# Entering the first round of a staged token-mixing kernel in eight steps instead of six

## The chip, the cores and the metric

The kernel runs on one NeuronCore of a Trainium2 chip. The metric is the device time of one execution in microseconds (us), taken as the median of several runs. The engines are called as the profile calls them: PE (TensorE, matrix products), DVE (VectorE), ACT (ScalarE), POOL (GpSimd) and SP (SyncE, which here only issues DMAs); "PEld" is PE's loading of weights.

## The reference

Eight sequences of 4224 tokens with 192 channels go through a causal seven-tap convolution, whose weights are a softmax per head, and then through a token-mixing layer:

```python
x  = causal_conv(x, softmax(weight))          # 8 heads of 24 channels, 7 taps
th = x @ w_theta
y  = einsum('ts,bsd->btd', w_tok_r, x*cos(th)) + einsum('ts,bsd->btd', w_tok_i, x*sin(th))
u  = x + y
out = u + relu(u @ w_ch)
```

Nearly all the arithmetic is in the two 4224 x 4224 token mixes, `w_tok_r` and `w_tok_i`, each applied to 8 x 192 = 1536 columns.

## The kernel before

**Tiles.** The 4224 input tokens are cut into 33 *chunks* (`NK`) of 128, and the 4224 output tokens into 33 *row blocks* of 128. Row blocks are handled in pairs, which gives 17 *units* (`NU`): 16 pairs and one single block. Every chunk must meet every unit once.

**What a chunk needs before it can be mixed** (class `Chunk`): its x tokens are loaded by POOL's queue, and a short history of 16 tokens per quarter is copied by SP's queue from the chunk before (tile `xw`); two convolutions on PE (`conv`, L216) with their evacuation by ACT or DVE; a store of the convolved x (`store`, SP); twelve PE transposes (`transpose`, L170); two channel mixes on PE (`theta`, L146), each followed by two sines on ACT (L291); two products on DVE (`product`, L297); four subtractions on DVE (`sums`, L306). The result, seven half-width operands, stays in SBUF in one of 11 `z` buffers (`NW` = 11).

**Steps.** Time is cut into *steps* (class `Step`). In a step one unit is mixed with all the chunks that are active in it, `n` of them. A chunk enters at step `start[k]`, stays for 17 steps, and then leaves its `z` buffer to the chunk that comes 11 later; so there are three *rounds* of 11 chunks. The list `start` decides how many chunks are active in each step. With

```python
base = [0, 0, 1, 1, 2, 3, 3, 4, 4, 5, 5]
start = [base[k % NW] + (NU + 1) * (k // NW) for k in range(NK)]
```

the first six steps have n = 2, 4, 5, 7, 9, 11, most steps have 11, and where one round gives way to the next n falls to 9 or 10 for six steps (17 to 22 and 35 to 40). The last five steps have 9, 7, 6, 4, 2. There are 58 steps, and `shift` puts the single block on the last one.

**The mix of one pair of row blocks** is a seven-product scheme: four token-weight tiles are turned on DVE from the loaded `st` (`turn`, L387) and four combinations of them are formed on DVE (`wsum`, L399); then seven *runs* of n *products* each go to PE, a product being two matmuls of 384 columns (L536). After each run the sum in PSUM is given to the row block's accumulator `pv` (`give`): by DVE (L461), or in the first round for four of the seven by ACT (L459). PSUM holds two such sums at a time. In steps 0 and 1 (`plain`) eight runs without combinations take the place of the seven.

**Between steps** the accumulators of a row block go to DRAM and come back 17 steps later (`part`, 768 KB each way per row block, SP's queue, L549 and L425). The token weights of step t+2 are loaded during step t (`load_w`, L374): four DMAs each for `w_tok_r` and `w_tok_i` on POOL's queue, into two `st` buffers. `xw` and `pv` share six buffers (tag `big`).

**The order of the work** is written by hand. `Step.mix` yields before every product, and at set places within the step (in sevenths of it) runs its events: the next step's turns and sums, loads, the tasks of the chunks that enter at the next step (`Chunk.tasks`, places in `step_events`), and outputs in the last 17 steps. The residual x is added to each row block once: by POOL in the step before a visit (`load_x`, `add_x`, L439) or by an accumulating DMA into `part` (`add_ahead`, L448). `quiet` says which visits of the second round may take it.

The first 11 chunks are not prepared through `step_events` but by the loop at the end of the kernel, its *entry passes* i = 1 to 12. Pass i issues the convolutions and transposes of chunk i and the channel mixes and products of chunk i-1, and between them calls `between`, which lets `more` take products from the stream of steps as long as these need no chunk above `ready[0]` = i-2. Before, a pass takes up to 11 products (2+1+2+1+2+1+1+1), and chunk i+3 is loaded in pass i, chunks 0 to 5 ahead of the passes. In pass 1, `idle` matmuls on noise keep PE busy.

Of the kernel before, what the change touches and what calls it, by code (L numbers as in the profile page):

```python
# [16 lines left out]
def kernel(  # L17
# [34 lines left out]
    NK = S // P  # L52
# [7 lines left out]
    NU = (NT + 1) // 2  # L60
    NW = 11
    PC = 512
    NP = 4

    base = [0, 0, 1, 1, 2, 3, 3, 4, 4, 5, 5]
    assert len(base) == NW
    start = [base[k % NW] + (NU + 1) * (k // NW) for k in range(NK)]
    NSTEP = start[-1] + NU
    shift = (NU - 1 - (NSTEP - 1)) % NU

# [14 lines left out]
    def pe(ins):  # L85
        return in_order("pe", ins)
# [96 lines left out]
    class Chunk:  # L183


        def __init__(self, k, before=None):
            self.k = k
            self.xw = wk.tile([2 * WR, 2, B, D], F16, name="xw", tag="big", bufs=6)
            for a in range(NQ):
                h, lo = a // 2, (a % 2) * WR  # L190
                t0 = token(k, a)
                hist = self.xw[lo : lo + HALO, h, :, :]
                if before is not None:
                    nc.sync.dma_start(  # L194
                        out=hist, in_=before.xw[lo + Q : lo + Q + HALO, h, :, :]
                    )
                elif t0 == 0:
                    nc.vector.memset(hist, 0.0)
                else:
                    lo, t0 = lo - HALO, t0 - HALO  # L200
                lo += HALO
                n = (a % 2 + 1) * WR - lo
                nc.gpsimd.dma_start(  # L203
                    out=self.xw[lo : lo + n, h, :, :],
                    in_=x[:, t0 : t0 + n, :].rearrange("b s d -> s b d"),
                )
# [117 lines left out]
    def load_chunk(k):  # L324
        if k < NK and k not in chunks:
            chunks[k] = Chunk(k, before=chunks[k - 1] if k % NW else None)

    def active(t):
        return [k for k in range(NK) if start[k] <= t < start[k] + NU]

    def unit(t):
        return (t + shift) % NU

    class Step:


        def __init__(self, t):
            self.t, self.u, self.ks = t, unit(t), active(t)
            self.n = len(self.ks)
            self.tbs = [tb for tb in (2 * self.u, 2 * self.u + 1) if tb < NT]  # L340
            self.pair = len(self.tbs) == 2
            self.first = t < NU
            self.final = t + NU >= NSTEP
            self.late = self.final and self.n < NW
            visits = [v for v in range(NU, NSTEP) if v % NU == t % NU]
            quiet = [v for v in visits if start[2 * NW - 1] < v <= 2 * NU]
            self.adds, self.ahead = [], []
            for i, tb in enumerate(self.tbs):
                known = self.known(tb)
                if t not in ([v for v in quiet if known < v - 1] or visits[-1:])[:1]:  # L350
                    continue
                if not self.late:
                    self.adds.append(i)
                else:
                    far = known <= start[2 * NW - 1]
                    self.ahead.append((i, 2 * NU - NW + 2 * (t % NU) if far else start[-1],
                                       (t // NU - 1 - far) % 2))
            self.plain = self.first and self.pair and self.n <= NP
            self.time = 0.324 * self.n * (8 if self.plain else 7 if self.pair else 5 if self.n <= 2 else 4)
            self.closing = False  # L360
            self.st, self.w, self.xr, self.ub, self.uT, self.pv = {}, {}, {}, {}, {}, []
# [274 lines left out]
    steps = [Step(t) for t in range(NSTEP)]  # L636
# [75 lines left out]
    for a in range(2):  # L712
        nc.gpsimd.affine_select(
            out=sel, in_=sel, pattern=[[1, Q - 1 + 2 * WR]], channel_multiplier=-1,
            base=-(Q - 1 + HALO - KS + 1 + a * WR), compare_op=ALU.not_equal, fill=1.0,
# [13 lines left out]
    def idle(n):  # L729
        for _ in range(n):  # L730
            pe(nc.tensor.matmul(
                spare[:, 0, 0:BH], lhsT=noise[:, 0:P], rhs=noise, start=True, stop=True
            ))
# [30 lines left out]
    for q in range(Q):  # L764
# [3 lines left out]
            start=True, stop=True,  # L768
# [16 lines left out]
    flow = stream()  # L785
    need = [None]

    def more(n):

        for i in range(n):  # L790
            if need[0] is None:
                need[0] = next(flow, NK)
            if need[0] > ready[0]:
                return n - i
            need[0] = next(flow, NK)
        return 0

    steps[0].load_rows()
# [4 lines left out]
    for m in (1, 2):  # L803
        steps[1].load_w(m)
    load_chunk(4)
    load_chunk(5)
    for g in range(NG):
        chunks[0].conv_batches(g)
    idle(2)
# [2 lines left out]
    for i in range(1, NW + 2):  # L812
        ch = chunks.get(i) if i < NW else None
        old = chunks[i - 1] if i <= NW else None

        def between(n):
            left = more(n)
            if i < 3:
                idle(min(left, 2) if i == 1 else 0)

        if ch:
            ch.conv(0)
        between(2)
        if old:
            old.theta(0)
        ready[0] = i - 2
        between(1)
        if ch:
            ch.conv(1)
        between(2)  # L830
        if old:
            old.theta(1)
        if i in (1, 3):
            for name in ("11", "21"):
                steps[i // 2].turn(name)
        if i + 3 < NW:
            load_chunk(i + 3)
        between(1)
        if i == 1:
            for first in (Z11, Z21):  # L840
                old.product(first, slice(0, 1))
        if ch:
            ch.transpose()
        if i == 1:
            for first in (Z11, Z21):
                old.product(first, slice(1, 2))
        elif old:
            old.product(Z11)
        between(2)
        if i > 1 and old:  # L850
            old.product(Z21)
        if i in (1, 3):
            for name in ("12", "22"):
                steps[i // 2].turn(name)
        between(1)
        if old and start[i - 1] > NPS:
            old.sums(0)
        between(1)
        if old and start[i - 1] > NPS:
            old.sums(1)  # L860
        between(1)
    ready[0] = NK
    for _ in flow:
        pass
# [31 lines left out]
```

## Time and profile before

| | us |
|---|---|
| median of 3 runs (1435.09 to 1443.39) | 1437.17 |
| the profiled execution | 1437.8 |
| its span, first to last instruction | 1436.0 |
| PE busy in the span | 1409.4 (98%) |
| DVE busy | 973.0 (68%) |
| POOL busy | 434.3 (30%) |
| ACT busy | 310.6 (22%) |

The profile is of one execution. Its time is 1.8 us longer than its span, and 0.6 us above the median of the runs. Line numbers such as L536 are lines of the kernel before. The granted PE clock was 0.999 on the mean. PE's busy time counts the whole latency of an isolated instruction, so a busy PE may still be issuing below its best rate. [...]

### The profile page before, as it was taken

What the parts mean: (1) busy time and instruction counts of PE and PEld (TensorE: products, weight loads), DVE (VectorE), ACT (ScalarE), POOL (GpSimd) and SP (SyncE); (2) the same over time, 40 slices, a digit from 0 to 9 for tenths busy, and PEclk for the clock granted to TensorE, in tenths of its full rate; (3) what the DMA queues carried; (4) which work ended last, traced back from release to release, by engine and by line L of the source; (5) the groups of instructions that cost most, each with busy time, mean ns of one, the idle gap of its engine ahead of it and who ended that gap; (6) DMA issues with size and microseconds to landing.
All of it is one profiled execution on the core that took longest, in us unless ns stands there. A gap on an engine that the chain in (4) does not pass through costs nothing.

```text
span 1436.0 us, 23771 instructions
## 1 busy us (share of the span) xinstructions
PE 1409.4 (98%) x9829; PEld 889.7 (62%) x9829; DVE 973.0 (68%) x1046; ACT 310.6 (22%) x374; POOL 434.3 (30%) x655
## 2 busy tenths in 40 slices
PE   8889999999999999999999999999999999999997
PEld 5556666666666666666666666666566666666665
DVE  6893554545548787866665657877777677767676
ACT  5851101111124244000000004335100110010133
POOL 8511211111233332532333343233323123213110
PEclk9999999999999999999999999999999999999999
DMA  9975766564799999898899889999999999999894
GB/s 193 234 164 132 147 125 128 100 151 89 147 232 227 231 236 239 209 256 177 232 236 229 229 157 243 231 198 255 248 206 216 215 206 220 203 202 197 166 214 136
DMA packets 272045, 281.99 MB, mean 196 GB/s; under 512 B 106688, under 2 KB 240192, under 8 KB 271936
## 3 DMA queue, kind: packets, MB, share of 16 engines
q0 software_dynamic: 162464, 92.15, 48.8%
q1 hardware_dynamic: 71840, 178.88, 35.4%
q10 hardware_dynamic: 37632, 9.44, 4.5%
q8 instruction: 77, 1.26, 0.4%
q14 instruction: 32, 0.26, 0.1%
HBM read 245.49 MB, written 108.13 MB: 246 GB/s over the span
## 4 chain that ended last, share of the span: by engine, by line
PE 92%; DMA 2%; DVE 2%; ACT 1%; SPq 1%; issue 1%; POOL 0%; DVEq 0%; ACTq 0%; POOLq 0%
PE y L536 84%; PE v L146 5%; PE tp L170 1%; PE pc L216 1%; ACT z L291 1%; DMA xw<-in_x_dram 1%; DMA xw<-xw 1%; SPq L194 1%; DVE pv L461 0%; DVE z L306 0%; DVE pv L585 0%; DMA part<-pv 0%; DMA st<-in_moe_w_tok_r_dram 0%; DMA wsb<-in_weight_dram 0%; DVE wt L399 0%
## 5 line engine op out<-in xcount | busy, mean ns | idle before, releaser
L536 PE MATMUL y<-z,wt 128*128 128x384 f16 x7672 | 1282.4, 326 | 6.4 <-DVE pv L461 5.3
L536 PEld LDWEIGHTS <-wt 128*128 128x128 f16 x7672 | 743.7, 98 | 482.6 <-issue 6.3
L461 DVE TENSOR_TENSOR pv<-y,pv 128x768 f32<-128x768 f32 x317 | 302.5, 954 | 323.9 <-PE y L536 284.0
L387 DVE STREAM_TRANSPOSE wt<-st 128x1408 f16<-128x1408 f16 (+7 forms) x224 | 327.5, 1465 | 51.0 <-PE y L536 38.3
L374 POOL DMA_DIRECT2D st<-in_moe_w_tok_r_dram x232 | 132.3, 578 | 463.5 <-DVE wt L387 451.8
L374 POOL DMA_DIRECT2D st<-in_moe_w_tok_i_dram x232 | 132.4, 579 | 405.0 <-DVE wt L387 396.5
L399 DVE TENSOR_TENSOR wt<-wt 128x1408 f16<-128x1408 f16 (+6 forms) x208 | 173.4, 834 | 40.5 <-PE y L536 38.3
L156 ACT ACTIVATE z<-pc 128x768 f16<-128x768 f32 (+1 forms) x62 | 47.5, 803 | 387.0 <-PE pc L216 378.4
L156 ACT ACTIVATE ub<-pv 128x768 f16<-128x768 f32 x63 | 50.2, 836 | 343.6 <-DVE pv L461 315.9
L459 ACT ACTIVATE pv<-y 128x768 f32<-128x768 f32 x66 | 53.7, 814 | 280.5 <-PE y L536 280.5
L146 PEld LDWEIGHTS <-uT 128*128 128x128 f16 x1056 | 90.6, 98 | 23.8 <-issue 5.9
L439 POOL TENSOR_TENSOR pv<-pv,xr 128x1536 f32<-128x1536 f32 x24 | 74.5, 3103 | 66.2 <-issue 26.7
L203 POOL DMA_DIRECT2D xw<-in_x_dram x132 | 76.3, 587 | 27.1 <-issue 7.0
L585 DVE SCALAR_TENSOR_TENSOR pv<-v,pv 128x768 f32<-128x768 f32 (+1 forms) x67 | 62.8, 942 | 24.9 <-PE v L146 24.5
L306 DVE TENSOR_TENSOR z<-z 128x768 f16<-128x768 f16 x132 | 71.2, 552 | 2.2
L291 ACT ACTIVATE z<-v,half_pi 128x768 f16<-128x768 f32 x66 | 59.6, 903 | 56.4 <-PE v L146 55.7
L156 ACT ACTIVATE uT<-tp 128x1536 f16<-128x1536 f16 (+1 forms) x47 | 56.5, 1208 | 47.3 <-PE tp L170 47.3
L297 DVE TENSOR_TENSOR z<-z 128x1536 f16<-128x1536 f16 (+1 forms) x68 | 60.6, 926 | 4.3 <-ACT z L291 4.2
L146 PE MATMUL v<-wth,uT 128*128 128x192 f16 x528 | 54.4, 246 | 2.7 <-ACT z L291 2.1
L146 PE MATMUL v<-wch,uT 128*128 128x192 f16 x528 | 54.3, 246 | 1.3 <-DVE pv L585 0.7
L291 ACT ACTIVATE z<-v 128x768 f16<-128x768 f32 x66 | 53.2, 806 | 0.0
L216 PE MATMUL pc<-xw,bands 96*64 96x192 f16 x512 | 30.4, 251 | 5.4 <-DMA st<-in_moe_w_tok_r_dram 2.7
(45 smaller groups left out, 144.8 us busy)
## 6 DMA issues: line engine op xcount, KB each, us to landing
part<-pv SPq DMA_DIRECT2D x79, 768.0 KB, 4.3
pv<-part SPq DMA_DIRECT2D x79, 768.0 KB, 6.0
out_dram<-pv SPq DMA_DIRECT2D x65, 384.0 KB, 4.5
st<-in_moe_w_tok_r_dram POOLq DMA_DIRECT2D x136, 176.0 KB, 6.0
st<-in_moe_w_tok_i_dram POOLq DMA_DIRECT2D x136, 176.0 KB, 5.3
xs<-z SPq DMA_DIRECT2D x132, 96.0 KB, 5.1
xw<-in_x_dram POOLq DMA_DIRECT2D x121, 96.0 KB, 6.2
xr<-xs SPq DMA_DIRECT2D x24, 384.0 KB, 4.5
```

Source lines behind the costliest of these rows:

```text
L146: pe(nc.tensor.matmul(v[:, k, b * D : (b + 1) * D], lhsT=tT[:, 3 * k + b + i, :], rhs=w[:, 2 * b + i, :], start=(i == 0), stop=(i == 1),))
L156: act(nc.scalar.activation(out=out, in_=in_, func=AT.Copy))
L203: nc.gpsimd.dma_start(out=self.xw[lo : lo + n, h, :, :], in_=x[:, t0 : t0 + n, :].rearrange("b s d -> s b d"),)
L291: act(nc.scalar.activation(**args))
L306: dve(nc.vector.tensor_tensor(out=z[:, o, :], in0=z[:, a, :], in1=z[:, b, :], op=ALU.subtract))
L374: pool(nc.gpsimd.dma_start(out=st[a * Q : (a + 1) * Q, 0:nb, :, 0:n] .rearrange("i r bt s -> i (r bt) s"), in_=w[self.tbs[0] * P : (self.t ...
L387: dve(nc.vector.transpose(self.w[name][:, 0 : self.n, :, :], self.st[int(name[1])][:, int(name[0]) - 1, :, 0 : self.n * Q] .rearrange("p b ...
L399: dve(nc.vector.tensor_tensor(out=self.w[name][:, 0 : self.n, :, :], in0=self.w[a][:, 0 : self.n, :, :], in1=self.w[b][:, 0 : self.n, :, : ...
L439: ins = pool(nc.gpsimd.tensor_tensor(out=self.pv[i], in0=self.pv[i], in1=self.xr[i], op=ALU.add))
L461: dve(nc.vector.tensor_tensor(out=o, in0=yv, in1=o, op=ALU.add))
L536: pe(nc.tensor.matmul(y[cn][:, q, 0:BH], lhsT=self.w[wn][:, c, :, :].rearrange("p bt i -> p (bt i)"), rhs=chunks[k].z[:, zn, q * BH : (q + ...
L585: dve(nc.vector.scalar_tensor_tensor(out=ub[:, ks, :], in0=v[:, ks, :], scalar=0.0, in1=ub[:, ks, :], op0=ALU.max, op1=ALU.add,))
```

## The change

The list `base` becomes one list per round. The first round enters two chunks in each of steps 0 and 1 and then one a step up to step 8; the second round enters over steps 20 to 26, the third over steps 39 to 44, and the last five steps have 9, 7, 6, 4, 2 chunks as before. There are 61 steps. The number of chunks per step becomes:

| steps | before | after |
|---|---|---|
| 0 to 8 | 2 4 5 7 9 11 11(single) 11 11 | 2 4 5 6 7 8 9 10 11 |
| 17 to 25 | 9 9 10 9 9 9 11(single) 11 11 | 9 7 6 7 8 8 9 10 10 |
| third round enters | 35 to 40: 9 9 10 9 9 9(single) | 37 to 43: 9 7 8 8 7 8 9(single) |

In the entry loop, a pass no longer takes up to 11 products. `reach(r)` gives the number of products of the stream that come before the first one that needs a chunk above r; pass i spreads the products from `reach(i-3)` to `reach(i-2)` over its eight calls of `between`, at the given thirteenths. Chunk 5 is no longer loaded ahead of the passes; from pass 3 on, pass i loads chunk i+2. Two lines that place the addition of the residual (`quiet`, `ahead`) are fitted to the new steps.

```diff
-    base = [0, 0, 1, 1, 2, 3, 3, 4, 4, 5, 5]
-    assert len(base) == NW
-    start = [base[k % NW] + (NU + 1) * (k // NW) for k in range(NK)]
+    bases = ([0, 0, 1, 1, 2, 3, 4, 5, 6, 7, 8],
+             [2, 2, 3, 3, 4, 5, 5, 6, 6, 7, 8],
+             [3, 3, 4, 4, 5, 6, 6, 7, 7, 8, 8])
+    start = [b + (NU + 1) * r for r, base in enumerate(bases) for b in base]
...
-            quiet = [v for v in visits if start[2 * NW - 1] < v <= 2 * NU]
+            quiet = [v for v in visits if start[2 * NW - 1] - 5 < v <= 2 * NU]
...
-                    self.ahead.append((i, 2 * NU - NW + 2 * (t % NU) if far else start[-1],
+                    self.ahead.append((i, start[2 * NW - 1] + 2 * (t - NSTEP + 6) if far else start[-1],
...
+    done = [0]
+    chunk_of = [s.ks[item[3]] for s in steps for item in s.products()]
+
+    def reach(r):
+
+        return next((i for i, k in enumerate(chunk_of) if k > r), len(chunk_of))
+
     def more(n):
...
             need[0] = next(flow, NK)
+            done[0] += 1
         return 0
...
-    load_chunk(5)
...
-        def between(n):
-            left = more(n)
-            if i < 3:
-                idle(min(left, 2) if i == 1 else 0)
+        lo, hi = reach(i - 3), reach(i - 2)
+
+        def between(n, upto):
+            left = more(max(0, round(lo + (hi - lo) * upto / 13) - done[0]))
+            if i == 1:
+                idle(min(n, 2))
...
-        if i + 3 < NW:
-            load_chunk(i + 3)
-        between(1)
+        if i > 2:
+            load_chunk(min(i + 2, NW - 1))
+        between(1, 4.5)
```

The other calls become `between(2, 0)`, `between(1, 1)`, `between(2, 3)`, `between(2, 6.5)`, `between(1, 8)`, `between(1, 9.5)` and `between(1, 11)`.

More of the change, by code (lines that the diff above doesn't have):

```diff
@@ L63 @@
     NP = 4
-    base = [0, 0, 1, 1, 2, 3, 3, 4, 4, 5, 5]
-    assert len(base) == NW
-    start = [base[k % NW] + (NU + 1) * (k // NW) for k in range(NK)]
+    bases = ([0, 0, 1, 1, 2, 3, 4, 5, 6, 7, 8],
+             [2, 2, 3, 3, 4, 5, 5, 6, 6, 7, 8],
+             [3, 3, 4, 4, 5, 6, 6, 7, 7, 8, 8])
+    start = [b + (NU + 1) * r for r, base in enumerate(bases) for b in base]
+    assert len(start) == NK and all(
+        start[k + NW] > start[k] + NU for k in range(NK - NW)
+    )
     NSTEP = start[-1] + NU
@@ L814 @@
         old = chunks[i - 1] if i <= NW else None
-        def between(n):
-            left = more(n)
-            if i < 3:
-                idle(min(left, 2) if i == 1 else 0)
+        lo, hi = reach(i - 3), reach(i - 2)
[3 more added lines that the diff above has]
+                idle(min(n, 2))
         if ch:
             ch.conv(0)
-        between(2)
+        between(2, 0)
         if old:
@@ L826 @@
         ready[0] = i - 2
-        between(1)
+        between(1, 1)
         if ch:
             ch.conv(1)
-        between(2)
+        between(2, 3)
         if old:
@@ L835 @@
                 steps[i // 2].turn(name)
-        if i + 3 < NW:
-            load_chunk(i + 3)
-        between(1)
+        if i > 2:
+            load_chunk(min(i + 2, NW - 1))
+        between(1, 4.5)
         if i == 1:
@@ L848 @@
             old.product(Z11)
-        between(2)
+        between(2, 6.5)
         if i > 1 and old:
@@ L854 @@
                 steps[i // 2].turn(name)
-        between(1)
+        between(1, 8)
         if old and start[i - 1] > NPS:
             old.sums(0)
-        between(1)
+        between(1, 9.5)
         if old and start[i - 1] > NPS:
             old.sums(1)
-        between(1)
+        between(1, 11)
     ready[0] = NK
```

## The prediction

> **What bounds the kernel now.** I read the page first. PE is busy 98% of the span, DVE 68%, and the slices show where PE is not full: at the start and at the very end.
>
> ```profile
> PE 1409.4 (98%) x9829; PEld 889.7 (62%) x9829; DVE 973.0 (68%) x1046; ACT 310.6 (22%) x374; POOL 434.3 (30%) x655
> PE   8889999999999999999999999999999999999997
> DMA  9975766564799999898899889999999999999894
> ```
>
> PE's rate when nothing holds it is in a steady stretch, the windows of line L536 alone (columns: stretch, its length, PE busy, count, clock, DMA share, GB/s):
>
> ```profile
> 150.00:400.00 250.00, 250.00 (x1540) 1.00 0.62 130
> ```
>
> 250 us / 1540 = 0.1623 us a matmul, so 0.325 us a product. Then the windows of the start:
>
> ```profile
> 20.00:40.00 20.00, 18.23 (x180) 12.06 (x175) 12.15 (x18) 16.78 (x21) 13.97 (x25) 1.00 1.33 229
> 40.00:60.00 20.00, 17.28 (x165) 11.35 (x166) 17.42 (x30) 16.67 (x21) 11.92 (x21) 1.00 1.25 219
> 60.00:80.00 20.00, 16.46 (x159) 11.22 (x159) 19.71 (x31) 16.38 (x21) 5.75 (x11) 1.00 1.10 245
> 80.00:100.00 20.00, 18.54 (x145) 11.76 (x143) 18.15 (x26) 13.52 (x17) 2.88 (x6) 1.00 0.81 179
> ```
>
> The columns are PE, PEld, DVE, ACT and POOL busy, clock, DMA share. PE idles 9.5 of these 80 us, while DMA is above 1 and DVE rises to 19.7 of 20. What ended PE's waits between 20 and 101 us, from the list of waits (us, times, longest):
>
> ```profile
> PE pc L216 <- DMA st<-in_moe_w_tok_r_dram: 2.7, 2, 2.3
> PE pc L216 <- DMA xw<-xw: 2.7, 2, 2.0
> PE y L536 <- DVE pv L461: 1.8, 1, 1.8
> ```
>
> Convolutions waited for data, and products for DVE. From 101 to 1000 us the same list has one PE wait, 1.8 us. So outside the entry passes (and about 3 us at 1000 to 1020, and the end) only removed PE work could help; the gap to close is in the passes.
>
> How large is it? The timeline of PE gives each piece by the distance to the next start:
>
> ```profile
> 28.29 0.82 PE L146 MATMUL v<-wth,uT 128*128 128x192 f16 x8
> 28.95 0.49 PE L536 MATMUL y<-z,wt 128*128 128x384 f16 x2
> 29.28 0.83 PE L170 MATMUL tp<-ident,z 128*128 128x128 f16 x12
> 29.95 2.04 PE L536 MATMUL y<-z,wt 128*128 128x384 f16 x10
> 31.92 0.58 PE L216 MATMUL pc<-xw,bands 96*64 96x192 f16 x8
> 32.43 0.82 PE L536 MATMUL y<-z,wt 128*128 128x384 f16 x4
> ```
>
> A channel mix takes 0.66 us, the transposes 0.67, half a convolution 0.46 to 0.51; a chunk is 2x0.66 + 0.67 + 0.97 = 2.96 us. Between 20 and 100.67 us, where the unbroken run of products begins, the trace has 236 product matmuls (118 products, 38.3 us) and nine chunks and a half of preparation (160 L146, 143 L216 and 108 L170: 28.0 us). 66.3 us of work took 80.7: **14.4 us are lost.** That is all the first part of the change can win.
>
> **Part 1, the entry passes.** Preparations and matmuls stay the same in number: 7672 product matmuls, since each chunk meets each unit once, steps 0 and 1 stay plain and the last step has n = 2. What moves is how many products lie in a pass. From the new `start`, passes 2 to 11 get 4, 20, 4, 24, 36, 43, 50, 57, 64, 71; before, at most 11. From pass 6 on, PE has 36x0.325 + 2.96 = 14.7 us and more a pass, against about 7 before. DVE in pass 6 has, by its rows' means, four turns and four sums for n = 6 (4x0.97 + 4x0.55), three gives of 0.95, one chunk's 2x0.95 + 4x0.55, and about 1 left over from the plain steps: 14 us. Its operations follow each other some 0.08 us closer than their means (a product of z at 50.36, the next operation at 51.23), which takes 1.2 off. So PE is the longer one by 2 us in pass 6, and by more in each pass behind it. What remains lost, pass by pass: pass 2 as now (conv of chunk 2 at 19.70 to conv of chunk 3 at 25.25 is 5.55 us for 4.26 of work: 1.3); pass 3 ends on step 1's turns, which ran at 32.76 (1.0); pass 4 has only 4 products and so pass 2's chain (1.3); pass 5 has 10.8 us of PE and 12.1 of DVE, sixteen operands of subtraction among it (1.3); pass 6 takes over DVE's lag (1.0); the rest 1.0. Sum 6.9, so **7.5 us won**. Bounds: only passes 2 and 4 lose (2.6, so 11.8 won), or a tenth of the passes is lost as in the 20 to 40 us row with all of the above (11, so 3.4 won).
>
> Chunk 5's load moves past the first convolutions and, on POOL, behind the first `st` of step 2; behind it wait that step's other `st` and DVE's turns of it. POOL spends 4x0.587 = 2.35 us on it and the median landing is 6.2; the rest of pass 3 and pass 4 cover 9.5. Chunks 6 to 10 are loaded a pass closer to their use than before, but the passes are at least twice as long. Nothing is taken for it; if the cover is gone it is at most the 2.3 us of the longest wait above, inside the bound.
>
> **Part 2, three more steps.** They add 3x7 = 21 gives on DVE (20.0 us), 12 turns and 12 sums, whose width in total is unchanged (about 0.15 us of fixed part each, from the means at 512 and 1408 columns: 3.6), 24 W issues on POOL (0.58 each: 13.9) and 6 `part` stores and loads. PE does none of it; while PE is full it is free. Three more POOL additions (27 for 24, 3.1 us each) take the place of six accumulating DMAs; nothing is taken for that trade.
>
> **Part 3, the round changes.** Here the cover is thinner: a step with n = 6 or 7 has less PE time but the same gives, entering chunks and `part` traffic. Per step, PE needs 2.27n + 2.96 per entering chunk. DVE needs seven gives (6.7), 8.2 for two chunks, four turns and four sums of the next step; less 0.08 an operation. DMA time, spread over 16 engines, from the trace's packets: W (the token weights) is 2048 packets a step whatever n is (82 ns at 704 B, 72 at 576, 62 at 448), so 10.5 us at n = 11, 9.3 at 9, 7.9 at 7; four `part` transfers of 128 packets of 267 ns, 8.5; a chunk 1024 packets of x of 53 ns, 3.4, and 192 of 147 ns for its store and history, 1.8.
>
> - Before, n = 9 with two entering: PE 26.4, DVE 21, DMA 28.2 (1.07 of PE).
> - After, step 18 (n = 7, none): PE 15.9, DVE 11.6, DMA 23.2 (the next two chunks' x in it). Step 19 (n = 6, two): PE 19.6, DVE 19.6, DMA 27.5. Step 20 (n = 7, two): PE 21.8, DVE 20.4, DMA 24.1. Steps 38 and 41 resemble step 20, with DMA 27.5 and 23.6; 21, 22, 39, 40 and 42 have 10% or more to spare on DVE. Loads run one to two steps ahead at most, since `pv` and `xw` share six buffers, so a step's excess is only partly spread.
>
> How PE takes such loads now:
>
> ```profile
> 440.00:460.00 20.00, 20.00 (x172) 13.27 (x170) 16.29 (x20) 9.12 (x10) 6.48 (x12) 1.00 1.18 287
> 900.00:920.00 20.00, 20.00 (x163) 13.36 (x162) 18.54 (x24) 9.17 (x12) 2.29 (x4) 1.00 1.06 245
> ```
>
> DVE at 93%, or DMA at 1.18, cost PE nothing. Steps 18 and 19 ask 50.7 us of DMA in 35.5 of PE, 1.43; the largest share on record is 1.33 (20 to 40 us), by which they take 38.1: 2.6 us. DVE's full step 19 and near-full 20, 38 and 41: 0.4 each, 1.6. The additions for steps 22 and 23 fall into steps 21 and 22: 0.4. **4.6 us lost**; bounds: nothing, as in the two rows, or rival A's 19.
>
> [...] L399 has a median of 881 ns and a maximum of 3016, about POOL's 3103 of an addition. [...] The packets above go from 72 to 62 ns between 576 and 448 B without a jump. [...]
>
> **Sum.** 1437.8 (profiled execution) - 7.5 + 4.6 = 1434.9; less the 0.6 by which that execution lies above the median: **1434.3 us**. The end is the same n by n, so 0 there.
>
> **Rivals.**
> A. *The round changes become the bound.* Steps 18 to 20 run at the 60 to 80 us row (DVE 19.71, PE 16.46: 20/16.46 - 1 = 21.5% of 57.3 us, 12.3), steps 21, 22, 38 and 41 (88.8 us) at the 80 to 100 row (7.9%, 7.0): 19.3 lost, 1437.2 - 7.5 + 19.3 = **1449**. For: DVE and DMA are both at their records together there. Against: the rows at 440 and 900. It decides from a loss of 14.7 on. 0.18.
> B. *The round changes are free*, since loads run ahead in step 17, where nothing enters, and the passes win 10: **1427**. 0.22.
> C. *The passes were not short of products* but of arrivals; the convolutions' 5.4 us of waits move with them, and 3 is won: 1437.2 - 3 + 4.6 = **1438.8**. 0.12.
> The forecast has 0.48.
>
> **How the numbers follow.** About 0.5%, 7.2 us, is what a measurement of this kernel tells from no change. Faster by more: B mostly and a little of the forecast, 0.23. Slower by more: A nearly whole and the forecast's edge, 0.19. Within: 0.58. The range: below, B with an unhurt front (11.8 - 1 = 10.8 won: 1426); above, 1446, which leaves out the upper half of A and little else.
>
> **What would show it.** Right: the passes' PE busy near 20 of 20 from about 55 us on, DVE below 18 there; n = 11 is reached after 363 products for 195 now; 7672 product matmuls, 338 gives on DVE. Steps 18 and 19 (about 408 to 444 us) show DMA above 1.2 and PE a few us short. Wrong: waits of L216 for `xw` beyond 60 us (C); PE waits on gives or `st` of over 10 us at 400 to 560 and 855 to 980 (A); none at all (B).

## The result and the profile after

The changed kernel takes **1480.33 us** (median of 4 runs, 1473.73 to 1480.42) against 1436.72 (4 runs, 1435.09 to 1443.39) for the kernel before, run beside it: a ratio of 1.028, 95% interval 1.024 to 1.033. It is slower by about 41 us, where the prediction had 1434.3 with a range of 1426 to 1446. The profiled execution took 1473.7 us with a span of 1472.0, 36.0 us longer than the span before; the numbers below explain those 36.0. The other three executions took 6.6 us longer than the profiled one, and no trace shows where. Lines of the changed kernel stand 4 below those of before: products are L540, DVE's gives L465, convolutions L220, the x load L207, the `st` load L378, the residual addition L443, the history copy L198.

The page, engines and slices:

```profile
PE 1421.4 (97%) x9829; PEld 893.3 (61%) x9829; DVE 996.8 (68%) x1091; ACT 309.8 (21%) x374; POOL 453.8 (31%) x676
PE   7899999999988989999999999989999999999997
DMA  9996565655899999899799869998999999999884
```

PE's instructions are the same 9829. Its row has four new 8s: from 405 to 478 us, from 515 to 552 and from 957 to 994. These are the round changes. The windows of the start, in the columns of before (PE, PEld, DVE, ACT and POOL busy, clock, DMA share, GB/s; the DMA share is the time of the packets over that of 16 engines, and of the 1.31 in the first row q0 makes 0.93 and q1 0.38):

```profile
20.00:40.00 20.00, 16.22 (x154) 10.70 (x153) 12.83 (x18) 13.23 (x17) 14.07 (x26) 1.00 1.31 237
40.00:60.00 20.00, 18.76 (x163) 12.05 (x161) 17.24 (x30) 16.41 (x22) 9.67 (x17) 1.00 1.29 273
60.00:80.00 20.00, 18.13 (x127) 10.80 (x125) 14.29 (x21) 9.59 (x13) 10.41 (x19) 0.91 1.07 199
80.00:100.00 20.00, 18.90 (x144) 11.73 (x143) 14.09 (x19) 9.91 (x14) 6.88 (x12) 1.00 0.97 190
...
420.00:440.00 20.00, 14.58 (x94) 8.67 (x93) 8.59 (x11) 1.51 (x2) 5.81 (x10) 0.83 1.05 206
440.00:460.00 20.00, 17.25 (x134) 11.57 (x132) 13.98 (x20) 10.49 (x12) 7.11 (x13) 0.91 0.79 153
```

DVE has come down to 14 of 20 between 60 and 100 us, as forecast, and yet PE isn't full. At 420 to 460 us PE has 31.8 of 40 us, DVE is far from its limit, and the DMA share is no more than 1.05. The clock column holds something that the prediction priced nowhere: 0.83 and 0.91. What ended PE's waits from 400 to 560 us:

```profile
PE pc L220 <- DMA xw<-in_x_dram: 8.4, 2, 5.4
PE y L540 <- DVE pv L465: 8.0, 7, 2.1
PE pc L220 <- DMA xw<-xw: 2.4, 1, 2.4
```

In the kernel before, PE has no wait at all from 395 to 570 us. Convolutions now wait for x. The largest of these waits, in the timelines of PE and of POOL (start, duration, then in brackets the idle time before it):

```profile
429.13 0.27 PE L220 MATMUL pc<-xw,bands 96*64 96x192 f16 x1
434.82 1.49 PE L220 MATMUL pc<-xw,bands 96*64 96x192 f16 x15 [5.42 <-DMA xw<-in_x_dram]
```

```profile
415.03 1.24 POOL L207 DMA_DIRECT2D xw<-in_x_dram  x2 [6.26 <-DVE wt L391]
417.40 2.28 POOL L378 DMA_DIRECT2D st<-in_moe_w_tok_r_dram  x4 [1.13 <-DVE wt L391]
424.23 2.29 POOL L378 DMA_DIRECT2D st<-in_moe_w_tok_i_dram  x4 [4.54 <-DVE wt L391]
426.50 1.25 POOL L207 DMA_DIRECT2D xw<-in_x_dram  x2
```

This is step 19, which prepares the first two chunks of the second round. Two of the first chunk's four x transfers are issued at 415, the other two only at 426.50, behind the `st` loads of another step, which stand ahead of them in POOL's queue and wait until DVE has turned the tiles in the buffer. The convolution wants them 2.6 us later. The first two had been held as well, by something else: in the trace's semaphore events POOL stands before them from 407.82 to 414.25 us, until a `part` store issued at 411.05 has landed at 414.22, which frees one of the six `big` buffers (the view puts this wait down to DVE).

In the kernel before, the x of the same two chunks was issued from 394.40 to 404.87, for convolutions at 415.70 and 423.11:

```profile
394.40 2.47 POOL L203 DMA_DIRECT2D xw<-in_x_dram  x4
401.91 1.18 POOL L203 DMA_DIRECT2D xw<-in_x_dram  x2 [5.04 <-issue]
403.65 1.22 POOL L203 DMA_DIRECT2D xw<-in_x_dram  x2 [0.56 <-DMA st<-in_moe_w_tok_r_dram]
```

The second chunk's convolution stands at the end of another chain (the chain of waits between 410 and 450 us, some lines left out):

```profile
428.91 0.97 DVE pv L465
...
429.90 7.81 DMA part<-pv
...
437.77 0.32 SPq L429
...
438.19 0.51 SPq L198
...
438.75 6.00 DMA xw<-xw
...
444.89 0.82 PE pc L220 x15
```

Half of the history copy (L198) stands on SP's queue behind two loads of `pv` (L429), the second of which waits for a `part` store that takes 7.81 us to land. The x that it copies had landed before 434.82, when the first chunk's convolution went on.

**Where the 36 us are.** From the trace's PE records I took each matmul's distance to the next start and subtracted its pace where nothing holds it (0.1623 us for a product matmul, 0.0825 for a channel mix, 0.0557 for a transpose, 0.0488 for a convolution); what is left is time lost, put to steps by counting product matmuls. Half clock counts as lost. The sums differ by 36.4 us between the two kernels, the spans by 36.0. All kernels of this document, in us:

| kernel | steps 0-15 | 16-30 | 31-46 | rest | all |
|---|---|---|---|---|---|
| before | 23.0 | 1.6 | 5.4 | 5.1 | 35.2 |
| after | 20.5 | 29.0 | 16.9 | 5.2 | 71.6 |
| passes_alone | 28.7 | 2.5 | 3.8 | 5.1 | 40.1 |
| list_alone | 23.8 | 31.7 | 23.0 | 5.2 | 83.7 |
| second_gentle | 20.5 | 8.5 | 47.7 | 5.2 | 81.9 |
| third_gentle | 21.5 | 50.0 | 11.6 | 5.2 | 88.3 |
| no_x | 19.7 | 17.5 | 9.3 | 5.2 | 51.7 |
| thin_gives | 20.0 | 30.3 | 20.9 | 5.2 | 76.3 |
| x_early | 20.9 | 18.7 | 7.6 | 5.2 | 52.4 |
| residual_late | 18.4 | 25.6 | 18.4 | 5.2 | 67.5 |
| early_late | 19.2 | 11.0 | 9.0 | 5.2 | 44.4 |
| early_late_thin | 19.0 | 4.3 | 2.9 | 5.2 | 31.3 |
| seven | 24.9 | 1.6 | 6.5 | 5.1 | 38.1 |
| double_pace | 24.0 | 1.6 | 3.8 | 5.1 | 34.5 |

In the changed kernel 15.0 us are lost in step 19, 3.6 in step 20, 8.0 in step 22, 9.7 in step 41. From 60 us to the last microseconds the clock was at half (0.5 in the records of the granted clock) for 27.3 us, in six stretches (at 66.9, 432.2, 445.8, 462.9, 520.9 and 985.1 us); in the kernel before there was none. Product matmuls inside these stretches started 0.320 us apart (the median of 46 distances) for 0.162 outside them. In 4.3 us of the half clock PE stood waiting anyway; half of the other 23.0, 11.5 us, is a direct loss, and it lies inside the table's numbers.

### The profile page after: what moved, and what is told of

The parts are those of the page before. It is cut to its first block, busy times and chain, and to the rows that moved or that the text cites. A ratio compares the mean times of both kernels' runs of the same rounds, so it can differ in the third digit from the quotient of the medians.

```text
span 1472.0 us, 23906 instructions
## 1 busy us (share of the span) xinstructions
PE 1421.4 (97%) x9829; PEld 893.3 (61%) x9829; DVE 996.8 (68%) x1091; ACT 309.8 (21%) x374; POOL 453.8 (31%) x676
## 4 chain that ended last, share of the span: by engine, by line
PE 79%; DMA 10%; DVE 5%; POOL 2%; issue 1%; ACT 1%; SPq 1%; DVEq 0%; POOLq 0%
PE y L540 73%; PE v L150 4%; DMA xw<-in_x_dram 4%; DMA xw<-xw 2%; DVE pv L465 2%; PE pc L220 1%; DMA uT<-ub 1%; DVE z L301 1%; DVE wt L391 1%; PE tp L174 1%; POOL xw L207 1%; DVE z L310 1%; POOL st L378 1%; ACT z L295 1%; DMA st<-in_moe_w_tok_r_dram 1%
## 5 line engine op out<-in xcount | busy, mean ns | idle before, releaser
L540 PE MATMUL y<-z,wt 128*128 128x384 f16 x7672 | 1292.4, 327 | 19.0 <-DVE pv L465 16.4
L540 PEld LDWEIGHTS <-wt 128*128 128x128 f16 x7672 | 745.8, 98 | 502.9 <-issue 27.5
L465 DVE TENSOR_TENSOR pv<-y,pv 128x768 f32<-128x768 f32 x338 | 322.5, 954 | 338.7 <-PE y L540 293.1
L391 DVE STREAM_TRANSPOSE wt<-st 128x1408 f16<-128x1408 f16 (+8 forms) x236 | 328.8, 1398 | 46.2 <-PE y L540 36.2
L378 POOL DMA_DIRECT2D st<-in_moe_w_tok_r_dram x244 | 139.7, 581 | 435.8 <-DVE wt L391 432.2
L378 POOL DMA_DIRECT2D st<-in_moe_w_tok_i_dram x244 | 139.7, 581 | 410.3 <-DVE wt L391 396.3
L403 DVE TENSOR_TENSOR wt<-wt 128x1408 f16<-128x1408 f16 (+7 forms) x220 | 174.3, 792 | 43.9 <-PE y L540 41.6
L443 POOL TENSOR_TENSOR pv<-pv,xr 128x1536 f32<-128x1536 f32 x27 | 84.2, 3120 | 78.0 <-DVE pv L589 38.9
L207 POOL DMA_DIRECT2D xw<-in_x_dram x132 | 76.8, 594 | 53.1 <-PE pc L220 18.0
L310 DVE TENSOR_TENSOR z<-z 128x768 f16<-128x768 f16 x132 | 76.3, 589 | 2.2
L220 PE MATMUL pc<-xw,bands 96*64 96x192 f16 x512 | 33.5, 261 | 17.5 <-DMA xw<-in_x_dram 12.3
```

Source lines behind the costliest of these rows:

```text
L207: nc.gpsimd.dma_start(out=self.xw[lo : lo + n, h, :, :], in_=x[:, t0 : t0 + n, :].rearrange("b s d -> s b d"),)
L310: dve(nc.vector.tensor_tensor(out=z[:, o, :], in0=z[:, a, :], in1=z[:, b, :], op=ALU.subtract))
L378: pool(nc.gpsimd.dma_start(out=st[a * Q : (a + 1) * Q, 0:nb, :, 0:n] .rearrange("i r bt s -> i (r bt) s"), in_=w[self.tbs[0] * P : (self.t ...
L391: dve(nc.vector.transpose(self.w[name][:, 0 : self.n, :, :], self.st[int(name[1])][:, int(name[0]) - 1, :, 0 : self.n * Q] .rearrange("p b ...
L403: dve(nc.vector.tensor_tensor(out=self.w[name][:, 0 : self.n, :, :], in0=self.w[a][:, 0 : self.n, :, :], in1=self.w[b][:, 0 : self.n, :, : ...
L443: ins = pool(nc.gpsimd.tensor_tensor(out=self.pv[i], in0=self.pv[i], in1=self.xr[i], op=ALU.add))
```

## The experiments

Where an experiment has one time, it is that of its profiled execution, and is set against the profiled 1473.7 of the changed kernel, whose other three runs took 1480.3 to 1480.4; differences of less than about 7 us are therefore read from the table above and not from the times. D is the theory that the new lists lose the time in the round changes, P that the new entry loop does.

**1 and 2. Each half of the change alone.** The new entry loop with the lists of before, then the new lists with the entry loop of before:

```diff
 # passes_alone, against after
-    bases = (...)
-    start = [b + (NU + 1) * r for r, base in enumerate(bases) for b in base]
+    base = [0, 0, 1, 1, 2, 3, 3, 4, 4, 5, 5]
+    start = [base[k % NW] + (NU + 1) * (k // NW) for k in range(NK)]
 # (quiet and ahead as before, too)
 # list_alone: before, with after's bases, quiet and ahead
```

> The list of starts, quiet and ahead are those of before (58 steps, n = 2 4 5 7 9 11, round changes at n = 9 or 10); the entry loop is that of the changed kernel (passes of 4, 20, 4, 24, 36, 1, 50, 1, 64, 1 products, chunk 5 loaded in pass 3). Theory D (the loss lies in the round changes, where n dips to 6 and 7): no loss there, PE loss of about 1 us in each round change as before, total 1432 to 1442. Theory P (the new entry loop and its later loads cost the time): most of the 36 us remains, 1460 or more.

Measured: 1444.08 us (1443.25 to 1446.54), 1.0057 of before, interval 1.0039 to 1.0074. It lies between the two expectations and much nearer to D's: the loop by itself costs some 8 us, 28.7 lost for 23.0 in the front. With two chunks entering at one step, the second one's pass gets hardly any product, and steps 4 and 5 lose 3.5 and 2.7.

> The new lists of starts (61 steps) with the entry loop of before (up to 11 products a pass, chunk 5 loaded ahead). Theory D: both round changes lose as in the changed kernel, some 45 us of lost PE time together for 6 before, and the passes about what they lost before: 1470 to 1482. Theory P: the loss is gone, 1437 to 1447.

Measured: 1485.86. The lists alone give the whole slowdown and more, 54.7 us lost in the two round changes for 7.0 before. D holds.

**3 and 4. One round change made shallow, the other deep.** The second round's list is what lies between: early, it leaves the first change shallow and makes the second one deep, and the other way round.

```diff
 # second_gentle
-             [2, 2, 3, 3, 4, 5, 5, 6, 6, 7, 8],
+             [0, 0, 1, 1, 2, 3, 4, 5, 6, 7, 8],
 # third_gentle
-             [2, 2, 3, 3, 4, 5, 5, 6, 6, 7, 8],
+             [3, 3, 4, 4, 5, 6, 6, 7, 7, 8, 8],
```

> The changed kernel, but the second round enters as the first did (18 + 0 0 1 1 2 3 4 5 6 7 8), so that n is 9 or 10 at the first round change; the third round then has to take up all the shift, and n dips to 9 7 6 5 6 7 7 8 9 at the second change. Theory D: the first change falls from 28.7 us of lost PE time to under 3, the second rises from 16.7 to 20 to 35; in total 1450 to 1465. If instead two or more chunks entering a step were what costs, not the dip, the first change (one or two a step) falls too but the second stays near 17.

> The changed kernel, but the second round takes up all the shift (18 + 3 3 4 4 5 6 6 7 7 8 8; n = 9 7 6 5 6 7 7 8 9 at the first change) and the third enters like it, with n = 9 9 10 9 9 9 at the second change. Theory D: the second change falls from 16.7 us of lost PE time to about 5, as before; the first stays at 28 or rises to 40; in total 1460 to 1475. A theory of a general slowdown from more steps (DVE gives, DMA) would leave the second change at 10 or more.

Measured: 1483.93 and 1490.38. The direction is as expected, the sizes are not. In second_gentle the first change falls from 29.0 to 8.5 us lost and the second rises from 16.9 to 47.7 (steps 38 and 39, with n = 5 and 6, lose 15.5 and 16.4). In third_gentle the first rises to 50.0 and the second falls to 11.6, of which 7.2 in step 44. The loss grows faster than the missing work, so spreading the same 33 entries otherwise between the rounds wins nothing. In second_gentle's first change a part of the 8.5 has no low n to blame. Its POOL, at that place:

```profile
532.80 0.58 POOL L207 DMA_DIRECT2D xw<-in_x_dram  x1
537.50 3.34 POOL L443 TENSOR_TENSOR pv<-pv,xr 128x1536 f32<-128x1536 f32 x1 [4.13 <-DMA xr<-xs]
540.79 1.73 POOL L207 DMA_DIRECT2D xw<-in_x_dram  x3
```

A residual addition that waits 4.13 us for its operand holds back the other three transfers of a chunk's x by 8 us. PE's next wait, of 2.06 us, is not for that x but for a give, which stands on DVE behind two products of `z`; beside the addition these two took 4.73 us, for 1.8 elsewhere. The changed `quiet` allows additions in the round change itself; that is the suspect of experiment 6.

**5. x out of the way, and DVE out of the way.** Rival theories for the round changes: X, convolutions wait for late x; G, products wait for DVE's gives, since seven gives a step stay while PE's part of a step shrinks.

```diff
 # no_x, in Chunk.__init__
+            if k >= NW:
+                self.xw = chunks[NW - 1].xw
+                return
 # thin_gives, in give
+                if NU < self.t < 45 and self.n < NW:
+                    o, yv = o[:, :, 0:1, :], yv[:, :, 0:1, :]
                 dve(nc.vector.tensor_tensor(out=o, in0=yv, in1=o, op=ALU.add))
```

> The changed kernel, but the chunks of the second and third round load no x and copy no history; their convolutions read chunk 10's tile, so this part of the computation is left out, and the two buffers that these loads take in a round change are not asked for (one is held by chunk 10's tile). Theory X (in the short steps the x tiles come late, since their loads stand in POOL's queue behind token weights and in line for the six shared buffers): the two round changes lose under 8 us of PE time together for 46, total 1430 to 1440. Theory G (seven gives and the other work of DVE fill a step of n = 6 or 7): nothing changes, 1465 to 1475.

> The changed kernel, but in the steps of the round changes (n below 11, steps 18 to 44) a give adds a quarter of its columns, so part of the sums is left out; DVE has some 0.6 us less for each of seven gives a step, 4 us of some 20. Theory G: the round changes' loss falls from 46 us to under 20, total under 1450. Theory X: it stays above 35, total 1463 to 1475.

Measured: 1453.96 and 1478.44. Without the loads of x, 19.9 us fewer are lost, less than X expected (26.8 stay in the round changes) and more than G did. Thinner gives alone win nothing: while the convolutions stand for x, DVE isn't what PE waits for (from 400 to 560 us 16.1 us of waits for x and 1.5 for gives). But in no_x the waits from 390 to 570 us are of another kind (its lines stand 3 further on):

```profile
PE y L543 <- DVE pv L468: 11.5, 6, 4.3
```

So both are there, one behind the other: x ends the waits first, and when it is taken away the gives do.

**6. x loaded earlier; residual additions later.** Both keep the whole computation. The load of a chunk, event 4.5 of the step two before its entry, goes to event 0.3; `quiet` goes back to its text of before.

```diff
 # x_early
-                found.append((4.5, lambda k=k: load_chunk(k)))
+                found.append((0.3, lambda k=k: load_chunk(k)))
 # residual_late
-            quiet = [v for v in visits if start[2 * NW - 1] - 5 < v <= 2 * NU]
+            quiet = [v for v in visits if start[2 * NW - 1] < v <= 2 * NU]
 # early_late: both
```

> The changed kernel with the chunk's load asked for at 0.3 sevenths of the step instead of 4.5, about half a step earlier. Theory X: the waits of convolutions for x go, the loss of the round changes falls from 46 us to 15 to 25, total 1443 to 1455; if the six buffers and not the place in the queue hold the load, it falls by less than 10. Theory G: unchanged, 1468 to 1478.

> The changed kernel with the bound of quiet as before (without the 5), so that no residual is added in steps 22 and 23; row blocks 25, 26 and 27 take theirs by accumulating DMAs again. Theory X with the single xr buffer as a second cause: step 22's 8.0 us of lost PE time fall to 2 to 5, steps 19 and 41 stay at 15 and 10, total 1467 to 1471. If the additions cost nothing: 1473 as the changed kernel.

> x_early and residual_late together: the chunk's load at 0.3 sevenths of the step, and no residual added in steps 22 and 23. Theory X (late x) with the additions as second cause: the first round change falls from 18.7 us of lost PE time in x_early to 10 to 13 (steps 22 and 23 go to under 2 each, 19 and 20 stay at 4.7 and 3.7), the second stays near 7, the clock no longer drops behind step 20; total 1442 to 1449. If the 7.8 us of step 23 in x_early have another cause, the total stays at 1452 or more.

x_early: 1454.49, 19.2 us below the changed kernel, with no work left out and as much as no_x. POOL and PE at the same place as above:

```profile
394.20 1.86 POOL L207 DMA_DIRECT2D xw<-in_x_dram  x3 [7.18 <-ACT pv L463]
398.07 2.29 POOL L378 DMA_DIRECT2D st<-in_moe_w_tok_r_dram  x4 [2.00 <-DVE wt L391]
406.84 2.29 POOL L378 DMA_DIRECT2D st<-in_moe_w_tok_i_dram  x4 [6.49 <-DVE wt L391]
409.12 2.90 POOL L207 DMA_DIRECT2D xw<-in_x_dram  x5
```

```profile
429.49 0.85 PE L220 MATMUL pc<-xw,bands 96*64 96x192 f16 x16
```

The last issue for step 19 now lies 17 us and more ahead of the convolution, which runs with its 16 matmuls together and no wait. Three of the four transfers of the second chunk's history move ahead of the `pv` loads, and the fourth comes in time behind them. POOL's queue doesn't follow the places of the events to the letter, since only the `st` loads are chained to each other (`pool`): three transfers of the first chunk stand ahead of `st` loads whose events lie a step earlier, the fourth behind them. These three were released when a `part` store issued at 390.28 had landed at 393.45, so a buffer held them here too, only a step earlier. The list of PE's waits from 400 to 560 us has one line left:

```profile
PE y L540 <- DVE pv L465: 12.2, 8, 3.5
```

Half clock falls from 27.3 to 6.8 us, and no wait lies within the 6.8, so of the 19.2 us some 8 ((23.0 - 6.8) / 2) are the clock's and 11 are the waits themselves. The round changes keep 26.3 us, a little over the 15 to 25 expected.

residual_late: 1469.35, 4.4 us less than the profiled execution of the changed kernel; in the table 4.1 fewer lost. But 2.1 of these lie in steps 0 to 15, which the edit doesn't touch; the first round change loses 25.6 for 29.0, the second 18.4 for 16.9. early_late: 1446.47 (1446.06 to 1448.21), 1.0066 of before, interval 1.0051 to 1.0081; its loss is 8.0 below x_early's, nearly all in the first round change (18.7 to 11.0), where step 23 falls from 7.8 to under 1. So in the first round change the additions cost 3.4 us with x late and 7.7 with x on time. What DVE waited for in x_early from 515 to 560 us:

```profile
DVE pv L465 <- POOL pv L443: 6.2, 2, 4.2
DVE wt L391 <- DMA st<-in_moe_w_tok_i_dram: 4.8, 1, 4.8
```

Gives waited for the addition to the same accumulator, and a turn for token weights that POOL had issued right behind an addition, at 529.93. PE's longest wait there, 3.48 us that ended at 545.54, is for the give behind that turn, and 3.4 us of half clock follow it.

**7. The gives, with x on time.** thin_gives repeated on early_late:

> early_late, with gives of a quarter of the columns in the steps of the round changes (n below 11, steps 18 to 44), so part of the sums is left out. Theory G for the remainder (with x in time, DVE is what holds steps 19, 20, 38 and 41): their losses of 4.7, 3.7, 2.0 and 2.0 fall to under 1 each, and both round changes together to under 6. If short runs or DMA hold them, they stay above 10 together.

Measured: 1433.13, 13.3 us below early_late. The round changes lose 7.2 us for 20.0, a little over the expected 6 (step 19 keeps 2.9 of its 4.7), and about the 7.0 of the kernel before. No stretch of half clock is left after 60 us. The waits of PE on gives from 400 to 560 us, in early_late and then here (2 lines further on):

```profile
PE y L540 <- DVE pv L465: 6.8, 5, 2.1
```

```profile
PE y L542 <- DVE pv L467: 2.4, 2, 1.5
```

How a DVE that is 85% busy (17.06 of 20 us at 440 to 460) holds PE is seen in its timeline in early_late, and in PE's beside it:

```profile
440.00:460.00 20.00, 16.01 (x123) 9.70 (x123) 17.06 (x23) 6.72 (x8) 5.88 (x11) 0.91 1.11 270
```

```profile
447.50 1.81 DVE L301 TENSOR_TENSOR z<-z 128x1536 f16<-128x1536 f16 x2
449.24 1.14 DVE L310 TENSOR_TENSOR z<-z 128x768 f16<-128x768 f16 x2
450.30 0.95 DVE L465 TENSOR_TENSOR pv<-y,pv 128x768 f32<-128x768 f32 x1
```

```profile
447.11 2.11 PE L540 MATMUL y<-z,wt 128*128 128x384 f16 x12 [1.85 <-DVE pv L465]
451.30 0.48 PE L540 MATMUL y<-z,wt 128*128 128x384 f16 x2 [2.08 <-DVE pv L465]
```

With n = 6 a run of products lasts 2.11 us, and PSUM holds two sums. DVE ran its operations in the order of these lines, and an entering chunk's two products and two subtractions (2.9 us together) stood before the give. The run behind it began once the give was through, 2.08 us after PE had come free. With n = 9 a run lasts 2.9 us, about as long as those four operations.

**8. A middle course.** Eleven chunks over seven steps (59 steps), on early_late:

```diff
+    bases = ([0, 0, 1, 1, 2, 3, 4, 4, 5, 6, 6],
+             [0, 0, 1, 1, 2, 3, 4, 4, 5, 6, 6],
+             [1, 1, 2, 2, 3, 4, 4, 5, 5, 6, 6])
```

> early_late with a shift of one step instead of three: the first and second round enter in seven steps (0 0 1 1 2 3 4 4 5 6 6), the third with 1 1 2 2 3 4 4 5 5 6 6; 59 steps, n = 9 9 10 10 9 10 9 at the first round change and 9 7 8 9 8 9 9 at the second. By the theory of the dips the first change loses under 2, the second 3 to 6 us (before 5.4), the passes some 2 less than before; total 1432 to 1438, at best 0.3% faster than before. If the new passes cost more where two chunks enter in a step (as in passes_alone), 1438 to 1444.

Measured: 1442.56 (1439.94 to 1444.32), 1.0038 of before, interval 1.0023 to 1.0052, as the second of the two expectations had it. The round changes lose no more than before (1.6 and 6.5). What is left of the slowdown lies in the front: 24.9 for 23.0, with 3.6 in step 4 and 2.7 in step 6, where again two chunks enter at once.

**9. Were the passes short of products?** The kernel before, with up to 22 products a pass and nothing else changed:

```diff
-            left = more(n)
-            if i < 3:
-                idle(min(left, 2) if i == 1 else 0)
+            more(2 * n)
+            if i == 1:
+                idle(min(n, 2))
```

> The kernel before with its own lists and loads; only a pass may take up to 22 products instead of 11, so passes 5 to 11 have some 10 us of PE work for their DVE and DMA work instead of 7. If the passes of before lost time because too few products lay beside the chunks' preparation, the 10.4 us lost between 40 and 100 us fall to 5 to 7 and the total to 1431 to 1435. If arrivals and the chain of one chunk held them, nothing is won, 1436 to 1440.

Measured: 1437.41 (1431.88 to 1440.2), 0.9998 of before, interval 0.9984 to 1.0012. Two of its windows:

```profile
40.00:60.00 20.00, 17.94 (x140) 11.18 (x134) 16.25 (x28) 14.84 (x19) 10.35 (x19) 0.83 1.32 260
80.00:100.00 20.00, 20.00 (x175) 13.09 (x172) 17.46 (x23) 14.63 (x18) 4.56 (x8) 1.00 0.88 191
```

PE is full from 80 us on (18.54 before), but 8.5 us are lost in step 1 alone, where 6.8 us of half clock fall. More products a pass move the loss forward and win nothing that could be measured.

None of these kernels beats the one before with its whole work done.

## Why the prediction was wrong

The forecast was -7.5 in the passes and +4.6 in the round changes. Measured in the same profiled execution: about -3 and +39 (45.9 lost in steps 16 to 46 for 7.0). No run shows a term that would put the upper end of the range at 1446; the runs of the changed kernel took 1473.73 to 1480.42.

**Part 3 failed, the round changes.** Its working compared sums over a step, of DMA time and of DVE time, with PE's time of that step. What ran out was lead time and order. The experiments peel it off in turn, from 71.6 us lost: x and history on time -19.2 (x_early), additions out of the first round change -8.0 (early_late, 7.7 of it there), gives thinned -13.1 (early_late_thin), to 31.3, which is 3.9 below the kernel before. By its terms:

- *The loads of x* had no price in the round changes. The sentence "Loads run one to two steps ahead at most" was used against an excess of DMA time, and never turned into a time from issue to use. The view that had it is POOL's timeline of before: 21 us from the first issue to the convolution. The step whose event 4.5 issues this load had n = 11 before and has n = 7 now, so it is 4 x 2.27 = 9.1 us shorter; what POOL can issue only late in it comes too late for the use at the start of the next.
- *DMA, 2.6 us*, was to come from a share of 1.43 in steps 18 and 19. It was 0.88 in step 18 (412.8 to 428.7 us) and 0.96 in step 19 (428.7 to 462.8). In early_late, with x on time, it was 1.06 and 1.17, and PE's only waits were for gives; a loss by throughput isn't what the traces show. That the share in steps 18 and 19 would be over 1.2 was wrong.
- *DVE, 1.6 us* (0.4 each in steps 19, 20, 38 and 41): with x on time and the additions gone these steps lose 4.7, 3.6, 2.0 and 2.0, and thinner gives take 12.8 us from the two round changes. The mechanism was right, the size was 8 times too small. The two rows that were to bound it from below, DVE at 93% with PE full, were of steps with n of 9 or more; at n = 6 PE is held with DVE at 85%, because a run (2.11 us) is shorter than what stands ahead of a give (2.9 us).
- *Additions, 0.4 us*: 3.4 to 7.7 in the first round change. In the changed kernel two of the three there fell beside subtractions of `z` on DVE, whose maximum rose from 559 ns to 3327 (in residual_late it is 559 again) and whose total rose from 71.2 to 76.3 us. Two subtractions from 541.28 on took 3.92 us, for 1.14 elsewhere, beside an addition of 3.14 us that began at 541.05 (the two lines stand below). The subtractions held DVE about 5 us longer in all. That isn't the whole price: in x_early, where the additions cost most, no subtraction is longer than 560 ns, and the price came by the waits shown in experiment 6.
- *The clock* was not in the prediction. It takes 11.5 us of the 36, mostly behind the waits for x and its history.

```profile
541.05 3.14 POOL L443 TENSOR_TENSOR pv<-pv,xr 128x1536 f32<-128x1536 f32 x1
541.28 3.92 DVE L310 TENSOR_TENSOR z<-z 128x768 f16<-128x768 f16 x2
```

**Part 1 was mis-sized.** The passes' first convolutions stand at 18.12, 24.05, 35.40, 41.87, 53.06, 71.41 and 89.60 us. Against the prediction's work per pass, 2 to 7 lose 1.7, 1.9, 2.2, 0.4, 3.7 and 1.3 us, 11.2 in all for the forecast 6.9, so 3.2 were won for 7.5, just under the lower bound of 3.4. From pass 8 on PE is full, as said. Nine traces have this front; they lose 18.4 to 21.5 us in steps 0 to 15, 20.0 on the mean, for 23.0 before, which is 3 us as well. The missed terms are pass 6 (2.7 more than thought), where a wait of 1.87 us for a give at 66.70 is followed by 3.4 us of half clock, pass 3 (0.9) and the chains of the passes with 4 products (0.4 and 0.9); pass 5 lost 0.9 less. double_pace says the same from the other side: before, the early passes were not simply short of products, which speaks for rival C, though not by its mechanism. From 20 to 101 us the changed kernel has no PE wait on x or history. Why some 8 us are lost between 20 and 60 us in both kernels stays open. The one wait that the prediction counts from 101 to 1000 us is the 1.83 us that ended at 100.67, so behind the passes there was none.

**Part 2 was right.** 7672 product matmuls and 338 gives; DVE's gives cost 322.5 us for 302.5, turns and sums 2.2 more (3.6 forecast), `st` issues 279.4 for 264.7. In the full stretches and at the end PE lost nothing by it (5.2 for 5.1).

**The rivals.** A was the right direction, but it was priced by rows of the entry passes at 19.3 us, where 39 were lost; those rows had DVE full and the clock whole, and the loss came with neither. Its sign came in part: from 400 to 560 us PE waited 8.0 us on gives, not the 10 that A asked for, and 10.8 on `xw`. C's sign, L216 waiting for `xw` beyond 60 us, came there too and not in the passes that C was about. B falls.

What stays open: x_early moves the load in POOL's queue and also its claim on one of the six `big` buffers. The traces show both at work: of step 19's first chunk, two transfers were held for a buffer and the two that PE waited for behind `st` loads. What each is worth wasn't measured; a seventh buffer wasn't tried.

## What to carry to other kernels

When steps get shorter, whatever is issued "a step or two ahead" comes closer to its use in microseconds: for each DMA of a shortened step, compare the time from issue to use (2.6 us for the x issued at 426.50) with its landing time (5.7 us there), and count what waits ahead of it on its queue. Where one engine frees another's buffers, compare the longest burst that stands ahead of the freeing operation (2.9 us on DVE at n = 6) with the work that a buffer holds (2.11 us), and not the busy share (85%) with 100%. And price a new gap on PE above its own length where the clock can follow it down: here a gap of 1.87 us was followed by 3.4 us at half.

## What was not expected of the hardware

Gaps of about 2 us in PE's stream, which was otherwise full, were followed by half clock. After a wait of 1.87 us that ended at 66.70 the records show 3.4 us at half; the clock fell at 432.2, within the wait of 5.42 us that ended at 434.82, for 6.8 us; and again behind waits of 2.38 us to 444.89, 2.08 us to 462.84 and 2.96 us to 520.13, for 3.4 us each. In early_late two gaps of 1.85 and 2.08 us within 7 us were followed by 3.4 us. In the kernel before, gaps of 2.0 and 2.3 us in the entry passes (to 41.64 and 73.45) did not do it; what tells them apart stays open. Between 60 us and the last microseconds all stretches of the changed kernel and of early_late were about 3.4 or 6.8 us long; second_gentle and third_gentle have one of 10.2 us each.

The time of one x transfer from issue to landing, 6.2 us at the median before and 7.1 after, was 9.6 us and 10.9 us for the last ones of the loads that held steps 22 and 41. This isn't new in the changed kernel: before, the four transfers issued from 394.40 took 9.9 to 10.5 us, and four around 897 took 11.3 to 11.4. What changed is when they are issued: the last of step 22's at 510.5, for a convolution at 516.90.
